# Two thirds of one unit's x turned by DMA, with earlier loads around it, in a fused attention and feed-forward kernel

## The chip, the cores and the metric

The kernel runs on one core of a Trainium2 chip. The core has five engines that run side by side, each working through its own stream of instructions in order: TensorE (PE in the profile; PEld is its weight load), VectorE (DVE), ScalarE (ACT), GpSimd (POOL) and SyncE (SP). Here SP does no arithmetic: it issues almost all DMAs, one after the other. The transfers themselves are done by 16 DMA engines that all queues share. The metric is the device time of one execution in microseconds (us). The kernel before takes 326.93 us, the median of three runs (326.87 to 327.19).

## The reference

Two stages. The first is attention with 4 batches, 8 heads, 768 tokens and head size 64, where a query sees only the keys with the same 6-bit hash. The second is a gated feed-forward layer on 3072 tokens of 512 values, with 1536 inner values.

```
q_bits = (q @ proj > 0);  k_bits = (k @ proj > 0)          # 6 bits each
mask   = q_bucket[:, None] == k_bucket[None, :]
attn   = softmax(where(mask, q @ k.T / 8, -1e9));  o = attn @ v
x      = o with the heads side by side                     # 3072 x 512
xn     = x / sqrt(mean(x * x) + 1e-6) * rms_g
out    = (silu(xn @ w_gate) * (xn @ w_val)) @ w_out
```

## The kernel before, in words

**Units and slots.** The work is cut into 8 units u of 384 tokens (batch u // 2, one half of its queries). Each unit has 8 heads, and each head three chunks, so a unit has NS = 24 slots. In slot t the main loop emits the scores of chunk t + 1 (line 349, TensorE into a PSUM bank s_ps), the exponentials of chunk t (line 361, ACT), and then whatever the plan holds for the slot: a list of closures that `at(window, slot, function, ...)` fills while the kernel is written out. So the order of instructions on every engine, SP's too, is the order of the slots and, within a slot, the order of the `at` calls. Nothing is reordered later. Units 0 and 1 are mixed: heads 0 and 1 of both come first, then heads 2 to 7 of unit 0, then those of unit 1. From slot 48 on it is unit after unit.

**Pairs.** Heads are prepared two at a time, as a pair (batch, hp). `load_natural` (line 97), `load_blocks` (line 120) and `load_v` (line 106) load a pair's q, k and v from memory into tiles of one pool of 8 buffers (tag "L"); a load waits until the former user of its buffer has been read. load_blocks reads rows of 32 floats, eight DMAs a pair. The pair is turned so that the head size lies on the partitions, on TensorE for batch 0 and pairs (1, 0) and (1, 1), on DVE (lines 188 and 195) for the rest. It is cast to half precision (lines 178 and 208) and hashed on TensorE (`hash_pairs`, `hash_one`). The signs of the hash, the bits, are copied by small DMAs on SP into rows 64 to 69 of the tile QK that the scores read (lines 277 and 308). v is cast by `v_prep` and summed by `v_sum` on POOL. `zero_rows` clears the upper half of a QK tile on POOL (line 146).

**Feed-forward.** When all heads of a unit have their output x (line 395), `norm` computes the reciprocal root (line 443, POOL) and scales x into xn in three thirds c of 128 tokens. Then xn is turned into xnT, of which the first layer's matmuls read all three thirds at once. There are two ways:

- `turn_x`: four TensorE transposes into a PSUM bank x_ps (line 467), then a multiply by the column of weights gcol into xnT on DVE (line 473). For this third norm scales by the root alone (line 460).
- `turn_dma`: one DMA transpose on SP (line 431). The weights must be in already, so norm multiplies by the row of weights `grow` as well (line 452). `grow` is loaded once, the same 2 KB to each of the 128 partitions (line 673), and multiplied by a constant on ACT (line 674).

`ONDMA` says how many thirds of a unit go by DMA: two for units 2 to 6, one for unit 7, none for units 0 and 1. Unit u's norm stands at slot 24 (u + 1) + 4, its DMA turns one slot later.

Then the gate and value matmuls (line 484, banks g_ps and v_ps) run over 12 blocks of 128 inner values, with a tanh on ACT (line 492) and two multiplies on DVE (lines 501 and 502) for each, and the projection of the former unit (line 513, y_ps), copied out by ACT (line 525) and stored by SP (line 526). `spread` lays these pieces over the slots of a unit by written-down weights. A third that goes by DMA keeps its weight as an empty piece there, except in the last unit. The weights wg, wv and wo are loaded by DMAs that POOL issues (line 585).

**What the planner sets for the bits.** `hash_one` is put into the plan by `spread`; the bits' DMAs follow in its slot, or in a later one if `SENDS` names it. `spots` gives for each pair from (1, 2) on the slot of its loads, of its turns, and of its hash.

The lines that set the slots of what is changed:

```python
    ONDMA = {2: 2, 3: 2, 4: 2, 5: 2, 6: 2, 7: 1}
    ...
    at(0, 60, nc.sync.dma_start, grow, moe_rms_g.partition_broadcast(128))
    at(0, 65, nc.scalar.mul, grow, grow, float(DMODEL) ** 0.5)
    ...
        for c in range(ONDMA.get(u, 0)):
            at(0, t0 + 5, turn_dma, u, c)
```

Of the kernel before, what the change touches and what calls it, by code (L numbers as in the profile page):

```python
# [19 lines left out]
DMODEL = H * D  # L20
# [13 lines left out]
def kernel(  # L34
# [12 lines left out]
    nc = tc.nc  # L47
# [27 lines left out]
    grow = const.tile([128, DMODEL], FP32, name="grow")  # L75
# [347 lines left out]

    rstds = {}

    ONDMA = {2: 2, 3: 2, 4: 2, 5: 2, 6: 2, 7: 1}

    def turn_dma(u, c):
        if c == 0:
# [16 lines left out]
    def norm(u):  # L446
# [3 lines left out]
        for c in range(3 if 0 < u < 7 else 2):  # L450
            if c < ONDMA.get(u, 0):
                nc.vector.scalar_tensor_tensor(
# [145 lines left out]
    def at(w, s, f, *a):  # L598
        plan[NS * w + s].append(lambda: f(*a))
# [70 lines left out]
    at(0, 1, load_natural, nc.sync, 0, 3, "q")  # L670
    at(0, 2, load_v, nc.sync, 0, 2)
    at(0, 2, load_v, nc.sync, 0, 3)
    at(0, 60, nc.sync.dma_start, grow, moe_rms_g.partition_broadcast(128))
    at(0, 65, nc.scalar.mul, grow, grow, float(DMODEL) ** 0.5)
    at(0, 6, v_prep, 0, 1)
    at(0, 15, v_prep, 0, 2)
    at(0, 19, v_prep, 0, 3, nc.vector)
# [6 lines left out]
        at(0, 39 + 3 * i, load_w, wo, moe_w_out, 6 * i, 6)  # L684


    for hp, ts in ((0, (8, 22, 23, 24, 25, 24, 39, 26, 28, 42)), (1, (20, 27, 28, 29, 30, 29, 41, 32, 33, 43))):
        tl, ts = ts[0], ts[1:]
        for w in "kq":
            at(0, tl, load_natural, nc.sync, 1, hp, w)  # L690
        at(0, tl, load_v, nc.sync, 1, hp)
        at(0, ts[0], new_pair, 1, hp)
        for t, hh, w in zip(ts[0:4], (0, 1, 0, 1), "kkqq"):
            at(0, t, turn_pe, 1, hp, hh, w)
        at(0, ts[4], cast_pool, 1, hp, "k")
        at(0, ts[5], cast_pool, 1, hp, "q")
        if hp == 0:
            at(0, ts[6], hash_pair, 1, hp)
            at(0, ts[7], send_pair, 1, hp)
        at(0, ts[8], v_prep, 1, hp)  # L700
        at(0, ts[8], v_sum, 1, hp)
# [1 line left out]
    spots = {  # L703
        (1, 2): (34, (48, 48), (46, 46), 51),
        (1, 3): (45, (55, 56), (57, 58), 61),
        (2, 0): (50, (63, 64, 65, 66), (67, 69, 70, 71), 73),
        (2, 1): (62, (72, 73, 75, 81), (82, 83, 84, 85), 86),
        (2, 2): (70, (87, 88, 89, 90), (91, 93, 94, 95), 97),
        (2, 3): (84, (96, 97, 99, 105), (105, 106, 106, 107), 108),
# [2 lines left out]
        (3, 2): (114, (135, 136, 137, 139), (140, 141, 142, 143), 145),  # L712
        (3, 3): (132, (144, 145, 147, 153), (153, 154, 154, 155), 156),
    }
    for i, t in ((0, 39), (1, 41), (2, 57), (3, 61)):
        at(0, t, zero_rows, i)
    TX = 37

# [16 lines left out]
    for n, (u, h) in enumerate(order):  # L735
        t = 3 * n + 4 - ((u, h) == (0, H - 1))
# [52 lines left out]
            inserts[2 * b * NS + s] = (MEAN, v_mean, b, hp, 4)  # L789


    SENDS = {(2, 0, 0): 77, (2, 0, 1): 77, (2, 2, 1): 101, (3, 2, 1): 149}

    def place(t, step):
        if step[0] is None:
# [2 lines left out]
        if step[0] is hash_one:  # L798
            late.append((t, hash_bits, *step[1:]))
            for pair in step[1:]:  # L800
                for hh in range(2):
                    s = SENDS.get((*pair, hh), t)
                    late.append((max(s, t), send_bits, *pair, hh))
# [26 lines left out]
    for u in range(7):  # L830
# [9 lines left out]
        at(0, t0 + 4, norm, u)  # L840
        for c in range(ONDMA.get(u, 0)):
            at(0, t0 + 5, turn_dma, u, c)
        pieces = []
        for i in range(9):
# [5 lines left out]
            if i in (6, 7):  # L850
                thirds = ((0,), (1, 2))[i - 6]
                for c in thirds:
                    if c >= ONDMA.get(u, 0):
                        pieces.append((TURN, False, [(0, turn_x, u, c)]))
# [10 lines left out]
    def behind_norm(t):  # L865

        return t - t % NS + 9 if 1 <= t % NS < 9 else t

    for (b, hp), (load, kturns, qturns, _) in spots.items():
        at(0, load, load_blocks, nc.sync, b, hp)  # L870
        at(0, load, load_v, nc.sync, b, hp)
        at(0, min(kturns + qturns), new_pair, b, hp)
        for w, turns in (("k", kturns), ("q", qturns)):
            for i, t in enumerate(turns):
                at(0, t, turn_dve, b, hp, w, i, len(turns))
            t = turns[-1] + 1
            at(0, t if (b, hp) == (1, 2) else behind_norm(t), cast_pool, b, hp, w)
        t = 54 if (b, hp) == (1, 2) else behind_norm(qturns[-1] + 2)
        at(0, t, v_prep, b, hp)
        at(0, t, v_sum, b, hp)  # L880

# [66 lines left out]
```

## Time and profile before

| | |
|---|---|
| median of three runs | 326.93 us |
| the profiled execution | 326.68 us |
| its span, first to last instruction | 324.9 us |
| granted TensorE clock | 0.999 |
| TensorE busy | 319.9 us, 98% of the span |
| ACT, DVE, POOL busy | 228.4, 229.7, 157.6 us |
| DMA | 32.63 MB moved, 85741 packets, 70908 of them under 512 bytes |

How to read it: the page has the busy time of each engine, then 40 slices of the span (8.1 us each), where a digit is the busy share in tenths. The chain follows the work that ended last back to its start. A timeline gives start, duration, engine, line, operation, output and input, and how many instructions are merged in the row; for SP (written SPq) a row is the issue of a DMA, not its transfer. Matmuls overlap on TensorE and their ends are modelled, so the distance between starts is what counts. The table of stretches gives the busy time of each engine in each stretch, the clock, the mean busy share of the 16 DMA engines (a little over 1 where packets overlap) and GB/s.

### The profile page before, as it was taken

The numbers are of one execution on the slowest core, as the hardware profiler recorded it, in microseconds if no ns is written. First come the engines' busy times: TensorE is split into PE (matmuls) and PEld (weight loads), VectorE is DVE, ScalarE is ACT, GpSimd is POOL, SyncE is SP. The second block draws the span as 40 slices with busy tenths as digits, with TensorE's granted clock in tenths as the row PEclk, the third lists the DMA queues.
The fourth block names the chain that finished last, engine by engine and source line by source line (L and its number), as shares of the span: only waits on it lengthen the run. The fifth ranks groups of instructions, "written<-read, shape, count | busy, mean of one in ns | idle before, by whom it ended". The sixth has DMA issues, their size and how long they took to land.

```text
span 324.9 us, 7772 instructions
## 1 busy us (share of the span) xinstructions
PE 319.9 (98%) x2955; PEld 194.4 (60%) x2955; DVE 229.7 (71%) x512; ACT 228.4 (70%) x333; POOL 157.6 (49%) x204
## 2 busy tenths in 40 slices
PE   8999999999999999999999999999999999999996
PEld 3676666656566565655566565655666556665554
DVE  5887876859888568874888568785677536673870
ACT  7999887667688676776767776777777768744322
POOL 4999759955974363731883621752582111221000
PEclk9999999999999999999999999999999999999999
DMA  7942999988428864055547056002100030003002
GB/s 208 360 168 85 226 216 195 192 159 151 103 38 158 157 136 88 6 94 156 89 100 145 35 125 120 7 5 66 72 4 3 1 99 34 0 2 105 10 2 97
DMA packets 85741, 32.63 MB, mean 100 GB/s; under 512 B 70908, under 2 KB 82632, under 8 KB 85704
## 3 DMA queue, kind: packets, MB, share of 16 engines
q1 hardware_dynamic: 81800, 27.35, 36.1%
q0 software_dynamic: 3680, 4.72, 8.5%
q8 instruction: 23, 0.38, 0.5%
q14 instruction: 14, 0.11, 0.1%
q10 hardware_dynamic: 224, 0.07, 0.1%
HBM read 28.58 MB, written 6.29 MB: 107 GB/s over the span
## 4 chain that ended last, share of the span: by engine, by line
PE 98%; ACT 1%; DVE 0%; issue 0%
PE s_ps L349 20%; PE g_ps L484 19%; PE v_ps L484 19%; PE y_ps L513 18%; PE o_ps L374 11%; PE d_ps L218 2%; PE t_ps L156 2%; PE d_ps L238 2%; PE z_ps L580 1%; PE x_ps L467 1%; PE y_ps L532 1%; PE m_ps L333 1%; ACT psb L361 1%; DVE kT L158 0%; PE s_ps L156 0%
## 5 line engine op out<-in xcount | busy, mean ns | idle before, releaser
L361 ACT ACTIVATE psb<-s_ps,ebias 128x768 f16<-128x768 f32 x192 | 167.7, 900 | 20.0 <-PE s_ps L349 19.2
L349 PE MATMUL s_ps<-QK 128*128 128x384 f16 (+1 forms) x384 | 93.5, 326 | 1.2 <-ACT psb L361 1.1
L492 ACT ACTIVATE t<-g_ps 128x384 f32<-128x384 f32 x96 | 47.2, 492 | 52.2 <-PE g_ps L484 50.5
L484 PE MATMUL g_ps<-xnT,wg 128*128 128x384 f16 x384 | 82.7, 326 | 0.0
L484 PE MATMUL v_ps<-xnT,wv 128*128 128x384 f16 x384 | 81.8, 326 | 0.0
L501 DVE SCALAR_TENSOR_TENSOR a<-t,g_ps 128x384 f32<-128x384 f32 x96 | 53.0, 552 | 28.9 <-ACT t L492 27.2
L395 POOL TENSOR_TENSOR x<-otmp,rcp 128x384 f32<-128x384 f32 x30 | 25.1, 837 | 96.2 <-DVE rcp L393 95.8
L513 PE MATMUL y_ps<-wo,ht 128*128 128x512 f16 x276 | 67.7, 379 | 0.0
L502 DVE SCALAR_TENSOR_TENSOR ht<-a,v_ps 128x384 f16<-128x384 f32 x96 | 53.2, 554 | 11.5 <-PE v_ps L484 3.6
L374 PEld LDWEIGHTS <-psb 128*128 128x128 f16 x1152 | 51.9, 97 | 15.7 <-issue 1.2
L374 PE MATMUL o_ps<-vl,psb 128*128 128x65 f16 x1152 | 55.8, 193 | 0.0
L349 PEld LDWEIGHTS <-QK 128*128 128x128 f16 (+1 forms) x384 | 34.8, 98 | 33.7 <-issue 7.9
L484 PEld LDWEIGHTS <-wg 128*128 128x128 f16 x384 | 35.2, 97 | 21.2
L484 PEld LDWEIGHTS <-wv 128*128 128x128 f16 x384 | 35.1, 97 | 20.8 <-issue 0.2
L513 PEld LDWEIGHTS <-ht 128*128 128x128 f16 x276 | 24.9, 98 | 23.0
L525 ACT COPY ysb<-y_ps 128x512 f32<-128x512 f32 x23 | 13.5, 587 | 15.8 <-PE y_ps L513 15.8
L388 DVE TENSOR_TENSOR otmp<-o_ps,cvb 128x390 f32<-128x390 f32 x32 | 17.8, 557 | 7.1 <-PE o_ps L374 7.1
L208 POOL CAST QK<-qT 64x768 f16<-64x768 f32 x20 | 16.5, 823 | 10.3 <-DVE qT L195 9.5
L401 POOL TENSOR_TENSOR sq<-x 128x384 f32<-128x384 f32 x24 | 19.9, 828 | 1.9
L208 POOL CAST QK<-kT 64x768 f16<-64x768 f32 x20 | 16.4, 822 | 5.2 <-DVE kT L195 3.1
L473 DVE TENSOR_TENSOR xnT<-x_ps,gcol 128x512 f16<-128x512 f16 x11 | 7.4, 688 | 15.1 <-PE x_ps L467 15.0
L195 DVE STREAM_TRANSPOSE kT<-kL 128x192 f32<-128x192 f32 x32 | 16.4, 516 | 0.0
(85 smaller groups left out, 274.9 us busy)
## 6 DMA issues: line engine op xcount, KB each, us to landing
vn<-in_v_dram SPq DMA_DIRECT2D x16, 384.0 KB
out_dram<-ysb SPq DMA_DIRECT2D x23, 256.0 KB
qL<-in_q_dram SPq DMA_DIRECT2D x40, 96.0 KB
kL<-in_k_dram SPq DMA_DIRECT2D x40, 96.0 KB
kn<-in_k_dram SPq DMA_DIRECT2D x5, 384.0 KB
qn<-in_q_dram SPq DMA_DIRECT2D x5, 384.0 KB
wg<-in_moe_w_gate_dram POOLq DMA_DIRECT2D x2, 768.0 KB, 9.4
wv<-in_moe_w_val_dram POOLq DMA_DIRECT2D x2, 768.0 KB, 11.7
```

Source lines behind the costliest of these rows:

```text
L208: nc.gpsimd.tensor_copy(QK[b, 2 * hp + hh, "h"][0:64, o : o + S], src[64 * hh : 64 * hh + 64, :])
L349: nc.tensor.matmul(ps[:, j, 0:HALF], QK[b, h, "h"][rows, S + jt * 128 : S + (jt + 1) * 128], QK[b, h, "h"][rows, half * HALF : (half + 1) ...
L361: nc.scalar.activation(psb[u, h][:, 2 * ch : 2 * ch + 2, :], sps.pop((u, i))[:, :, 0:HALF], AF.Exp, bias=ebias, scale=ESCALE,)
L374: nc.tensor.matmul(o[:, c, hh, 0:65], psb[u, h][:, jt, c * 128 : (c + 1) * 128], vls[b % 2][:, h, 2 * (jt % 3) + jt // 3 if b in PARITY el ...
L388: nc.vector.tensor_add(tmp[:, :, :, 0:65], o[:, :, :, 0:65], cvb[b % 2][:, 2 * hp : 2 * hp + 2, 0:65].unsqueeze(1).to_broadcast([128, 3, 2 ...
L395: eng.tensor_mul(xd.rearrange("p c (h d) -> p c h d", h=2), tmp[:, :, :, 0:64], r.to_broadcast([128, 3, 2, 64]),)
L401: eng.tensor_mul(sq, xd, xd)
L484: nc.tensor.matmul(ps, w[:, kt, fs], xnT[u][:, kt, :], start=(kt == 0), stop=(kt == 3))
L492: nc.scalar.activation(t, fbank[u, ft, "g_ps"], AF.Tanh, scale=0.5)
L501: nc.vector.scalar_tensor_tensor(out=a, in0=t, scalar=1.0, in1=g, op0=ALU.add, op1=ALU.mult)
L502: nc.vector.scalar_tensor_tensor(out=ht[u][:, ft, :], in0=a, scalar=0.5, in1=vv, op0=ALU.mult, op1=ALU.mult)
L513: nc.tensor.matmul(y, ht[u][:, ft, c * 128 : (c + 1) * 128], wo[:, ft, :], start=(ft == 0), stop=(ft == NF - 1),)
```

## The change

Seven things, all of them slots but the first:

- `ONDMA` gets unit 1: two of its three thirds are turned by DMA, in slot 53, and scaled by grow.
- grow, which unit 1 now needs, is loaded in slot 40 in place of 60, and multiplied in slot 49 in place of 65.
- The loads of pair (1, 1) go from slot 20 to slot 17, ahead of the bits of pair (0, 3).
- The loads of pair (2, 0) go from slot 50 to slot 49, which puts them ahead of the store of unit 0's first third.
- The zeroing of QK tile 3 goes from slot 61 to 69.
- The bits of pair (1, 2) are sent in slots 53 and 54, behind unit 1's DMA turns, in place of slot 51.
- v_prep and v_sum of pair (1, 2) go from slot 54 to 57.

```diff
-    ONDMA = {2: 2, 3: 2, 4: 2, 5: 2, 6: 2, 7: 1}
+    ONDMA = {1: 2, 2: 2, 3: 2, 4: 2, 5: 2, 6: 2, 7: 1}
...
-    at(0, 60, nc.sync.dma_start, grow, moe_rms_g.partition_broadcast(128))
-    at(0, 65, nc.scalar.mul, grow, grow, float(DMODEL) ** 0.5)
+    at(0, 40, nc.sync.dma_start, grow, moe_rms_g.partition_broadcast(128))
+    at(0, 49, nc.scalar.mul, grow, grow, float(DMODEL) ** 0.5)
...
-    for hp, ts in ((0, (8, 22, 23, 24, 25, 24, 39, 26, 28, 42)), (1, (20, 27, 28, 29, 30, 29, 41, 32, 33, 43))):
+    for hp, ts in ((0, (8, 22, 23, 24, 25, 24, 39, 26, 28, 42)), (1, (17, 27, 28, 29, 30, 29, 41, 32, 33, 43))):
...
-        (2, 0): (50, (63, 64, 65, 66), (67, 69, 70, 71), 73),
+        (2, 0): (49, (63, 64, 65, 66), (67, 69, 70, 71), 73),
...
-    for i, t in ((0, 39), (1, 41), (2, 57), (3, 61)):
+    for i, t in ((0, 39), (1, 41), (2, 57), (3, 69)):
...
-    SENDS = {(2, 0, 0): 77, (2, 0, 1): 77, (2, 2, 1): 101, (3, 2, 1): 149}
+    SENDS = {(1, 2, 0): 53, (1, 2, 1): 54, (2, 0, 0): 77, (2, 0, 1): 77, (2, 2, 1): 101, (3, 2, 1): 149}
...
-        t = 54 if (b, hp) == (1, 2) else behind_norm(qturns[-1] + 2)
+        t = 57 if (b, hp) == (1, 2) else behind_norm(qturns[-1] + 2)
```

On SP the order around the turns becomes: bits of (1, 1), grow, the loads of (1, 3), the loads of (2, 0), the store of unit 0's first third, the two DMA turns, four bits of (1, 2), a store, the other four bits, a store. TensorE loses eight transposes and keeps the order of everything else.

## The prediction

> **What bounds the kernel now.** I read the page first: busy time, slices, chain.
>
> ```profile
> PE 319.9 (98%) x2955; PEld 194.4 (60%) x2955; DVE 229.7 (71%) x512; ACT 228.4 (70%) x333; POOL 157.6 (49%) x204
> ...
> DMA  7942999988428864055547056002100030003002
> ...
> PE 98%; ACT 1%; DVE 0%; issue 0%
> ```
>
> TensorE works in order and without holes, so the time is the sum of its work plus any wait put into its stream. DVE, ACT and POOL have room. The DMA engines are full from about 32 to 81 us (slices 5 to 10, 8.1 us each): that is where the change adds a transfer and puts two urgent ones in the queue.
>
> Next TensorE's timeline where unit 1's x is turned (x_ps) and first used (g_ps), and, last two lines, the same place of unit 4, which turns two thirds by DMA already:
>
> ```profile
> 75.09 0.39 PE L467 MATMUL x_ps<-ident,xn 128*128 128x128 f16 x4
> 75.32 1.03 PE L513 MATMUL y_ps<-wo,ht 128*128 128x512 f16 x4
> ...
> 76.78 0.74 PE L467 MATMUL x_ps<-ident,xn 128*128 128x128 f16 x8
> 77.36 0.49 PE L349 MATMUL s_ps<-QK 128*128 128x384 f16 x2
> ...
> 78.82 0.49 PE L484 MATMUL g_ps<-xnT,wg 128*128 128x384 f16 x2
> ...
> 190.97 0.44 PE L374 MATMUL o_ps<-vl,psb 128*128 128x65 f16 x9
> 191.39 0.81 PE L484 MATMUL g_ps<-xnT,wg 128*128 128x384 f16 x4
> ```
>
> Starts count, not modelled ends. Four transposes take 0.23 us, the next eight 0.58 (0.13 of it a wait for a bank). The gate matmul at 78.82 is the first reader of unit 1's xnT: it stands in TensorE's order, and all scores, probabilities and projections behind it stand with it.
>
> Then SP's queue, which issues one DMA after the other; the last line is unit 4's pair of DMA turns:
>
> ```profile
> 70.23 0.39 SPq L526 DMA_DIRECT2D out_dram<-ysb  x1
> 70.72 3.46 SPq L120 DMA_DIRECT2D qL<-in_q_dram  x4
> 74.28 2.65 SPq L120 DMA_DIRECT2D kL<-in_k_dram  x4
> 77.04 0.58 SPq L106 DMA_DIRECT2D vn<-in_v_dram  x1
> 77.72 5.75 SPq L308 DMA_DIRECT2D QK<-bits  x8
> 83.58 0.86 SPq L526 DMA_DIRECT2D out_dram<-ysb  x2
> 84.49 0.46 SPq L599 DMA_DIRECT2D grow<-in_moe_rms_g_dram  x1
> ...
> 187.45 2.58 SPq L431 DMA_TRANSPOSE xnT<-xn  x2
> ```
>
> At 74 us, when unit 1's xn will be ready, SP is in the middle of pair (2,0)'s loads. Unit 4 gives the price of a DMA turn: first issue at 187.45, reader at 191.39, 3.94 us; the reader could have come at 191.24, as the nine short matmuls before it take 0.27, so it waited 0.15 us and 3.94 is the turn's own length.
>
> Last the stretches of the DMA (columns: busy us of each engine, clock, DMA share, GB/s):
>
> ```profile
> 26.00:30.50 4.50, 4.08 (x60) 3.25 (x58) 3.08 (x8) 4.50 (x6) 4.08 (x6) 1.00 0.07 14
> 30.50:34.00 3.50, 3.50 (x50) 2.33 (x49) 2.56 (x6) 2.87 (x5) 3.14 (x4) 1.00 1.02 336
> 34.00:42.00 8.00, 8.00 (x111) 5.44 (x110) 7.28 (x24) 7.52 (x9) 5.63 (x7) 1.00 1.14 196
> 59.50:64.40 4.90, 4.90 (x46) 3.07 (x45) 4.10 (x8) 3.32 (x6) 4.59 (x8) 1.00 1.18 196
> 64.40:72.00 7.60, 7.60 (x67) 3.89 (x66) 4.92 (x14) 5.56 (x8) 4.55 (x6) 1.00 0.84 132
> 86.00:88.50 2.50, 2.50 (x35) 1.24 (x32) 2.32 (x5) 1.49 (x2) 2.32 (x4) 1.00 0.63 103
> ```
>
> From 30.5 to 34 the loads of pair (1,1) run, then the weights; from 59.5 to 64.4 the last half of wo, in which SP's own queue moves next to nothing; 86 to 88.5 is grow alone.
>
> **Part 1, eight transposes off TensorE.** Twelve cost 0.23 + 0.58; four stay at 0.23. Saved 0.58 us, or 0.46 if the bank wait stays. Two multiplies out of PSUM (L473, 0.69 us each) leave DVE, and two xn go from L460 to L452 (0.75 us); DVE is not on the chain, nothing is saved there. The weights in the planner stay, so no other matmul moves.
>
> **Part 2, the turns' wait.** The two turns stand behind pair (2,0)'s vn and the store of (0,0). DVE is not what they wait for: the reciprocal root ends at 73.35, two L452 at 0.75 us end at 74.9. SP is. Before, vn's issue ends at 77.62. The store (0.49 with its gap) moves from in front of the (2,0) loads to behind them: nil for the turns. grow goes in ahead: its issue costs 0.5. Its transfer can cost more: by the trace's semaphore records the store before it landed at 86.57 and grow at 88.66, so it held the engines 2.1 us. The stretch 64.4 to 72 has 16% of 7.6 us free, 1.2 us, to swallow it in. I take 0.9, between 0.5 and 2.1. The Trainium skill ("DMA: Bandwidth & Descriptors", section on the anatomy of one DMA) fits a DMA issued by GpSimd as 2.0 us plus bytes over 436 GB/s, so 0.6 us of moving for grow's 256 KB. By that sentence the sum below would be 0.3 lower; no run here shows grow moving so fast.
>
> So the first turn is issued at 77.62 + 0.9 = 78.5 and the gate can start at 78.5 + 3.94 = 82.45. Without a wait it would start at 78.82 - 0.58 + 0.2 (part 3) = 78.45. The wait is 4.0 us, in TensorE's stream, and nothing behind it has a hole to give it back. Low end: if the weights start 0.8 us sooner (part 3) and grow costs 0.5, 2.8 us. High end: grow's whole 2.1, 5.2 us.
>
> **Part 3, pair (1,1) loaded from slot 17.** SP is idle from 23.97 (four bits from 21.12, 2.85 us) to 26.30; the three loads now go there, at about 24.0, 24.5 and 25.0, instead of 29.18 to 30.60. Their 1.18 MB leave a full stretch (30.5 to 34) for an empty one. But the weights were not waiting for them: POOL issues the first at 30.27 and its packets start at 33.6 by the trace's packet records, 3.3 us later, where the last half of wo, with no loads before it, takes 2.6 (56.66 to 59.3). So at most 0.8 us is gained, and that last half keeps its time, since POOL issues it at 56.66. I take none of it, and keep 0.8 for the low end. The bits of pair (0,3), issued at 26.30 as before, now follow these loads in the rings. Pair (1,0)'s loads landed up to 4.31 us after vn's issue, so this vn lands at 29.3; bits that came behind a load (pair (0,1)) landed 0.2 and 0.4 us after it. Then k and q bits land at 29.5 and 29.7, where scores of head 6 start at 29.36 and the q bits landed at 28.85 before. Bounds: 0 (pair (0,2)'s bits landed 1.9 us after issue although a load landed just before) and 0.65 (vn 4.56 after issue, as pair (1,1)'s own was). I take 0.2.
>
> **Part 4, what has cover.** grow's multiply on ACT (0.64 us) comes at 66.1: grow lands at 65.5 to 67.5, and a wait of 1.4 us ends before the scores of 69.66 need the bank; beyond 2 us it would show. Bits of (1,2): issued from 81.1 on (78.5 + 2.58), 0.7 us each, the first three landed by 84.3; scores of unit 2's head 4 now come at 82.34 - 0.4 + 4.0 = 85.9; cover 1.6. Bits of (1,3) and the later loads follow DVE and TensorE, which shift too. POOL: v_prep and v_sum of (1,2) (2.8 us) leave the idle time at 73.3 and fall behind a memset at 81.9, so (1,3)'s casts end 2.8 later, at 90.9, where scores read them at 91.9 before the wait is added; without the wait the margin is about 0.5, with it 4. The memset of slot 69 (2.65 us) was at 91.0 and goes later; scores read its tile from slot 102 on (149 us).
>
> **Sum.** 326.68 (profiled execution; 324.9 of it is span) - 0.58 + 0.2 + 4.0 = 330.3. That execution lies 0.25 under the median of 326.93, so about 330.5 as a median.
>
> **Rivals.** (a) The turns come in time. The place is SP at 74 us; it decides at a first turn issued by 78.45 - 3.94 = 74.5, 4.0 us sooner than I say. It would need the moved 1.18 MB to pull the whole queue forward (at 336 GB/s, 3.5 us) and grow to vanish in it. For it: the DMA is full for 45 us, and in a full stretch bytes taken away come back as time. Against: those bytes lay before the weights, not between them, and wo's last half is timed by POOL. Time: 326.68 - 0.58 + 0 to 0.2, plus 0.25: 326.35 to 326.55, and slightly faster or the same by the measurement, which tells 0.2% (0.65 us) from no change. (b) The queue comes forward part of the way, by 1.5 to 3 us: wait 1 to 2.5, 327.5 to 329. (c) More is late: grow's 2.1 us in full, or longer as its reads meet wo's, the store's 256 KB in the rings ahead of the turns as well (0.7), or the bits of (0,3) at 0.65: 332.2 to 333.5.
>
> **How the numbers follow.** The order in SP's queue is certain, and it was busy until 77.62; so my case (wait 2.8 to 5.2, 329.3 to 331.7) gets 0.73, (a) 0.10, (b) 0.08, (c) 0.09. The range 327.9 to 332.3 leaves out (a) and most of (c). Slower: 0.73 + 0.08 + 0.09 = 0.90; of (a), 0.03 faster and 0.07 the same.
>
> **What would show it.** Right: in TensorE's timeline a hole of some 4 us before the first g_ps of unit 1, and four x_ps matmuls in front of it in place of twelve; SP's queue with the pair of turns at 78 to 79, directly after the store behind vn; ACT and DVE idle at 79 to 82; nothing else new past 85 us. Loads of (1,1) at 24 to 25.4 and the weights' packets starting no sooner than 32.8. A hole of 0.2 us before the scores at 29.4. Wrong: turns issued by 75 us, which would mean that the queue was held by those loads after all; or a hole elsewhere, at 29 us (bits), 67 us (ACT waiting for grow) or 91 us (POOL's casts).

## The result and the profile after

The changed kernel takes 334.39 us (median of four runs, 333.06 to 335.45); the kernel before, beside it on the same chip, 326.96. The ratio is 1.0218, with a 95% interval of 1.0200 to 1.0236. The forecast was 330.5, with a range of 327.9 to 332.3: the direction was right, the size was not. The profiled execution of the changed kernel took 333.79 us, its span is 332.0.

First the page of the changed kernel: busy time, three rows of its slices (8.3 us each), the chain, and from the groups the gate's matmuls with their idle time in front.

```profile
PE 322.0 (97%) x2947; PEld 195.0 (59%) x2947; DVE 227.7 (69%) x510; ACT 228.0 (69%) x333; POOL 156.9 (47%) x204
...
PE   9998999995899999999999999999999999999996
...
PEclk9999999999799999999999999999999999999999
DMA  7945999999105948026475237101300030002002
...
PE 95%; ACT 2%; DMA 1%; DVE 1%; issue 0%; DVEq 0%
...
L484 PE MATMUL g_ps<-xnT,wg 128*128 128x384 f16 x384 | 83.5, 328 | 4.4 <-DMA xnT<-xn 4.4
```

TensorE has eight matmuls less and yet 2.1 us more of busy time (322.0 against 319.9). The slices say why: the digit 5 at 75 to 83 us is the expected hole, and in the slice behind it the granted clock is 7 in place of 9. TensorE's timeline at that place shows both:

```profile
77.63 0.39 PE L467 MATMUL x_ps<-ident,xn 128*128 128x128 f16 x4
...
78.46 1.03 PE L513 MATMUL y_ps<-wo,ht 128*128 128x512 f16 x4
83.85 0.79 PE L484 MATMUL g_ps<-xnT,wg 128*128 128x384 f16 x2 [4.37 <-DMA xnT<-xn]
84.43 0.85 PE L349 MATMUL s_ps<-QK 128*128 128x384 f16 x2
85.07 0.85 PE L484 MATMUL g_ps<-xnT,wg 128*128 128x384 f16 x2
```

Four x_ps matmuls are left of twelve, as the change says. The projection's four matmuls are through at 79.31 (they are 0.21 us apart), and the gate starts at 83.85: a hole of 4.54 us. Behind it two matmuls of 384 columns take 0.64 us of starts (84.43 to 85.07) where they take 0.33 otherwise. The table of stretches for the hole, for what follows, and for the time after that (the columns are as before: us, PE, PEld, DVE, ACT, POOL, clock, DMA share, GB/s):

```profile
79.30:83.85 4.55, 0.18 (x1) 0.03 (x1) 1.55 (x4) 0.63 (x2) 3.42 (x3) 1.00 0.96 199
84.30:87.50 3.20, 3.20 (x13) 1.48 (x11) 0.82 (x2) 1.28 (x2) 2.98 (x5) 0.53 0.24 88
87.50:91.50 4.00, 4.00 (x41) 2.64 (x40) 3.34 (x6) 2.28 (x4) 2.03 (x4) 1.00 0.20 72
```

By the trace's clock records TensorE is granted half its clock from 83.90 to 87.32. SP's queue shows where the turns stand:

```profile
74.88 2.66 SPq L120 DMA_DIRECT2D kL<-in_k_dram  x4
77.64 0.58 SPq L106 DMA_DIRECT2D vn<-in_v_dram  x1
78.32 0.41 SPq L526 DMA_DIRECT2D out_dram<-ysb  x1
78.83 2.72 SPq L431 DMA_TRANSPOSE xnT<-xn  x2
```

Directly behind vn and the store, as forecast. By the trace's semaphore records vn landed at 82.02, the store at 82.76, the turns at 83.28 and 83.72. The bits of pair (0, 3) left a smaller hole in front of the scores of head 6, which started at 30.43 in place of 29.36.

To compare the two profiled executions I took the start of each slot's scores in both and noted where the distance between them changes:

| term | forecast | measured |
|---|---|---|
| start-up, first scores 6.86 to 7.29 | none | +0.42 |
| wait for the bits of (0, 3) | +0.2 | +0.69 |
| eight transposes | -0.58 | -0.57 |
| wait of unit 1's gate | +4.0 | +4.54 |
| half clock behind that wait | none | +1.68 |
| end of the program, behind the last matmul | none | +0.37 |
| sum | +3.6 | +7.1 |

The spans differ by 7.1 and the execution times by 7.11. The start differs by 0.25 to 1.10 us in the traces of all the variants below, whatever was changed; I count it as chance. SP's queue has a chance of its own on top of that. The run `end_two` below is the kernel before up to 248 us, and yet its v of pair (2, 0) was issued at 79.23 where the kernel before issued it at 77.04: 2.19 us later, with a start of TensorE only 1.10 later. So a difference of about 1 us between the holes of two single traces can be chance, and below it is called so.

### The profile page after: what moved, and what is told of

Its sections match the earlier page's. It is cut to its first block, busy times and chain, and to the rows that moved or that the text cites. A ratio compares the mean times of both kernels' runs of the same rounds, so it can differ in the third digit from the quotient of the medians.

```text
span 332.0 us, 7760 instructions
## 1 busy us (share of the span) xinstructions
PE 322.0 (97%) x2947; PEld 195.0 (59%) x2947; DVE 227.7 (69%) x510; ACT 228.0 (69%) x333; POOL 156.9 (47%) x204
## 4 chain that ended last, share of the span: by engine, by line
PE 95%; ACT 2%; DMA 1%; DVE 1%; issue 0%; DVEq 0%
PE s_ps L349 19%; PE g_ps L484 19%; PE v_ps L484 19%; PE y_ps L513 18%; PE o_ps L374 10%; PE d_ps L218 2%; PE t_ps L156 2%; PE d_ps L238 2%; ACT psb L361 1%; PE z_ps L580 1%; DMA xnT<-xn 1%; PE y_ps L532 1%; PE x_ps L467 1%; PE m_ps L333 0%; PE s_ps L156 0%
## 5 line engine op out<-in xcount | busy, mean ns | idle before, releaser
L473 DVE TENSOR_TENSOR xnT<-x_ps,gcol 128x512 f16<-128x512 f16 x9 | 6.1, 690 | 16.4 <-PE x_ps L467 16.4
```

## Experiments

The theory: TensorE waits for the turns, which come late because of what stands ahead of them in SP's queue; and the wait costs more than its length, since it is followed by half clock. The rivals: the matmuls behind the wait are slow for another reason (the transfers just landed, the banks); the turns are late because the DMA engines are full, not because of the order in the queue; something else that the change does sets the time.

**The half clock.** The changed kernel, with 17 matmuls of ones put in front of unit 1's first gate matmul. They write the next of the three banks that x_ps, y_ps, g_ps and v_ps take in turn, and nobody reads the result:

```diff
+            if u == 1:
+                warm = bank("z_ps")
+                idle(17, lambda name: warm)
```

> The changed kernel with 17 matmuls of ones (512 columns, 0.22 us each, 3.7 us in all, result not used) on TensorE directly before the first gate matmul of unit 1, where the changed kernel stands still for 4.54 us. After that hole its matmuls of 384 columns start 320 ns apart in place of 162 for some 3.4 us (granted clock 0.59 from 84 to 88 us), which costs 1.6 to 1.7 us. Theory A, the half speed comes from TensorE having been idle: the gate still starts when the DMA turns have landed, some 0.8 us of hole is left, but the half speed is gone, and the kernel is 1.7 us faster than the changed one, about 332.5 us. Rival B, the half speed has another cause (the DMA traffic, or this place of the program): it stays, and the time is that of the changed kernel, 333 to 335.5 us.

Measured 331.68 (331.63 to 332.07), ratio to the kernel before 1.0135 [1.0121, 1.0149], 2.7 us under the changed kernel. TensorE's timeline at the gate:

```profile
79.51 3.88 PE L583 MATMUL z_ps<-const-bfloat16-1.0 128*128 128x512 bf16 x17
83.34 0.48 PE L484 MATMUL g_ps<-xnT,wg 128*128 128x384 f16 x2
83.67 0.49 PE L349 MATMUL s_ps<-QK 128*128 128x384 f16 x2
```

and the stretch that answers to the slow one above:

```profile
83.50:87.50 4.00, 4.00 (x41) 2.63 (x40) 2.35 (x4) 2.37 (x4) 3.78 (x5) 1.00 0.21 75
```

The gate waits just as before, but TensorE is kept busy, the clock stays at 1.00, and scores are 0.33 us apart. The scores move by 3.83 us at this place where they moved by 6.21. Half clock after an idle TensorE is shown; the transfers and their order were the same, and the banks were taken in the same turn, one further on. The time lies 0.8 below what A expected: the profiled gate came 0.5 us sooner as well (83.34 for 83.85), which the fillers do not explain and which is within the chance of the queue. So of the 2.7 us some 1.7 belong to the clock.

**The order in SP's queue.** The changed kernel, with pair (2, 0)'s loads behind the turns and the bits of (1, 2), and its k issued before its q:

```diff
...
-        (2, 0): (49, (63, 64, 65, 66), (67, 69, 70, 71), 73),
+        (2, 0): (54, (63, 64, 65, 66), (67, 69, 70, 71), 73),
```

> The changed kernel with the loads of pair (2,0) in slot 54 in place of 49, so that they stand behind the DMA turns and the bits of (1,2) in SP's queue, and with that pair's k issued before its q. Theory A, the turns are late because SP and the rings are busy with these loads: first turn issued at about 75.5 us in place of 78.8, the gate no more than 0.6 us late, no half speed; 326.7 - 0.6 + 0.7 (bits of pair (0,3), as in the changed kernel) + 0 to 0.6, so 326.9 to 327.6 us. Rival B, a DMA turn is slow here for itself (rings full of other loads up to 76 us): the hole stays at 2 us or more, over 329 us.

Measured 332.44 (331.82 to 333.79), 1.0164 [1.0139, 1.0188]. The turns were issued at 75.31 and 76.74, both had landed by 79.17, and the gate did not wait: 3.86 us from first issue to last landing. So A was right at the gate; the time is nevertheless above 329, not for B's reason but because the lateness moved on. SP's queue in this kernel:

```profile
84.43 2.72 SPq L120 DMA_DIRECT2D kL<-in_k_dram  x4
87.25 2.66 SPq L120 DMA_DIRECT2D qL<-in_q_dram  x4
...
91.20 5.99 SPq L307 DMA_DIRECT2D QK<-bits  x8
```

TensorE's timeline there, and then the stretch behind it:

```profile
95.54 0.48 PE L348 MATMUL s_ps<-QK 128*128 128x384 f16 x2 [3.01 <-DMA QK<-bits]
```

```profile
97.00:100.00 3.00, 3.00 (x11) 1.37 (x9) 1.54 (x3) 1.32 (x3) 0.00 (x0) 0.50 0.42 66
```

Now the bits of (1, 3) stand behind the moved loads, scores wait 3.2 us for them, and half clock follows again.

**The early loads of (1, 1), alone.** The kernel before with nothing but slot 20 made 17:

> The kernel before with one change, the loads of pair (1,1) in slot 17 in place of 20. Theory A, as the trace of the changed kernel reads: a hole of 0.69 us before the scores of head 6 at 29.4 to 30.4 us, because the bits of pair (0,3) land behind the loads, and nothing given back: 327.6 us, 0.2% slower. Rival B, the weights and with them the rest of the queue come so much sooner that it is made up: 326.9 us or less.

Measured 328.23 (327.26 to 330.65, 12 runs) against 327.36, 1.0032 [1.0015, 1.0048]. The one new hole is 0.90 us before the scores of head 6; nothing later comes sooner. In this kernel, the changed one and its variants with slot 17 and grow in slot 40 this wait is 0.69 to 0.90, above the upper bound of 0.65 that I gave it.

**grow, first try.** The changed kernel with grow loaded in slot 20 in place of 40:

> The changed kernel with the load of grow in slot 20 in place of 40, where SP is idle and the DMA engines have not begun on the weights. It shows what grow costs the turns. If it costs its issue alone (0.5 us), the first turn is issued at 78.3 in place of 78.83 and the hole is 4.0 in place of 4.54; if its whole transfer (2.1 us), the first turn is issued at 76.8 and the hole is 2.5. The prediction took 0.9: hole 3.6. If the half speed after the hole needs a hole of a certain length, it may go here, for 1.7 us more: 330 to 333 us.

Measured 333.44 (332.88 to 334.07), 1.0186 [1.0170, 1.0203]. This is over what was expected, and it did not isolate grow: its transfer met the loads of (1, 1) and the bits of (0, 3), which landed at 31.6 to 32.2, so a hole of 2.03 us opened there, with half clock from 32.84 to 36.26. At the gate 2.78 us were left, with no half clock behind them (why, the last section says).

**The early loads undone in the changed kernel**, slot 17 back to 20:

> The changed kernel with the loads of pair (1,1) back in slot 20. Theory A (these loads in slot 17 only cost): the hole of 0.7 to 0.9 us before the scores of head 6 goes, the hole before the gate matmuls of unit 1 stays at 4.5 us (4 to 5.2), and so does the half speed after it: 0.8 us faster than the changed kernel, 333.2 to 333.8. Rival B (they also bring the queue forward): the hole before the gate grows by as much as they brought, up to 0.8 us, and the time is that of the changed kernel, 334.4.

Measured 334.78 (332.14 to 335.29), 1.0214 [1.0183, 1.0246]: no gain is seen, but this interval takes in the 0.8 us of A as well, so the time does not decide. The trace does in part. The hole at 29 us is gone, but the one before the gate is 5.97 us: TensorE comes to it 0.8 us sooner, and the turns land 0.6 us later (83.83 and 84.32), which alone would be within the chance of the queue. Half clock lasts longer too (2.5 us lost). A wait early in TensorE's stream is given back at a later one that is set by the queue.

**grow, second try**: the kernel just shown, with grow in slot 17, where SP is idle.

> As the run before, and grow loaded in slot 17 (SP idle at 24 to 26 us, DMA engines at 2 to 7%) in place of 40. It shows what grow costs the turns where nothing else moves. If its issue alone: the hole before the gate goes from 4.5 to 4.0 us. If its whole transfer: to 2.4. The prediction's middle value, 0.9: to 3.6. A hole of 0.1 to 0.5 at 29 us may come with it, since the bits of pair (0,3) follow grow. With the half speed 332 to 332.8 us, without it 330.5 to 331.5.

Measured 334.40 (332.83 to 335.27), 1.0214 [1.0190, 1.0238]. The hole before the gate is 5.26 in place of 5.97, and none opens at 29 us. The lengths expected were reckoned from the changed kernel's 4.5, while the kernel this one starts from has 5.97; what could tell is the difference of 0.7. But the turns land at 83.86 and 84.32, where they landed without the move (83.83 and 84.32), and TensorE's start is 0.71 later by chance, which is the whole difference. So neither try shows what grow costs ahead of the turns; with the chance of the queue at about 1 us, one trace each cannot.

**The loads divided.** The last kernel, with (2, 0)'s q left in front of the turns, then the turns, four bits of (1, 2), k, the other four bits, and v in slot 58:

```diff
...
+        split = (b, hp) == (2, 0)
-        at(0, load, load_blocks, nc.sync, b, hp)
-        at(0, load, load_v, nc.sync, b, hp)
+        at(0, load, load_blocks, nc.sync, b, hp, "q" if split else "qk")
+        if split: at(0, 53, load_blocks, nc.sync, b, hp, "k")
+        at(0, 58 if split else load, load_v, nc.sync, b, hp)
```

> As the run before, and pair (2,0)'s loads divided around the turns in SP's queue: q in slot 49, then the turns and four bits of (1,2), then k, the other four bits, v in slot 58, and then the bits of (1,3). Theory A (the whole loss at the gate is what stands ahead of the turns in SP's queue and in the rings): first turn issued at 75 to 75.5, gate waits 0 to 0.8 us, no half speed, bits of (1,3) as early as before: 326.4 to 327.3 us beside 326.9 to 327.4 of the kernel before, no measurable difference; the eight transposes saved (0.57 us) are about what is won. Rival B: a hole of 2 us or more stays at the gate or turns up at the scores of pair (1,3), over 329 us.

Measured 327.76 (326.61 to 330.23, 12 runs) against 327.38, 1.0019 [1.0002, 1.0035]. Against the kernel shown last, 6.6 us come back from the order in one queue alone, with the same bytes to move. The turns were issued 4.63 us sooner (75.15 for 79.78) and took 4.02 us to the gate in place of 4.67, while the DMA engines were busy for 0.72 of that time in place of 0.92. So most of the lateness is the place in the queue; full DMA engines are the smaller part of it. Left are a hole of 0.55 at the gate and one of 0.31 at 88 us.

**The turns in another engine's queue.** The changed kernel with slot 20, unit 1's turns issued by ACT in slot 55:

```diff
-        nc.sync.dma_start_transpose(
+        (nc.scalar if u == 1 else nc.sync).dma_start_transpose(
...
```

> The changed kernel with pair (1,1) in slot 20, and unit 1's two turns issued by ACT in slot 55 instead of SP in 53; SP's queue is as long as in the changed kernel. ACT reaches slot 55 at about 75.6 us. If only the place in SP's queue is late: turns issued at 75.6 and 76.9, landed by 79.3, hole before the gate 1 us, no half speed, 327.5 to 328.5 us. If the DMA engines themselves are what is late (full from 72 to 81 us): landing after 81, hole 2.5 us or more, 329.5 to 332 us. ACT is held 2.5 us by the issue itself, which delays the scores' bank at 79 us by up to 0.5 us in either case.

Measured 332.80 (331.76 to 333.02), 1.0160 [1.0141, 1.0178], over both forecasts. The turns were issued at 75.83 and 77.46 and landed by 80.27, and the gate's hole is 0.83, as if only the queue had been late. But in the trace's semaphore records SP then stands: a load of kL, queued at 76.40, waits for a DMA semaphore that one of ACT's turns is using, and goes on at 79.89, 0.02 us after that turn landed. The bits of (1, 2) behind it come late, and TensorE shows it:

```profile
86.61 0.48 PE L349 MATMUL s_ps<-QK 128*128 128x384 f16 x2 [2.52 <-DMA QK<-bits]
```

The hole is 2.69 us, with half clock behind it (87.40 to 90.82). A further 0.86 us of this execution is a wait at 68 us for the second half of wo, which stands in no other trace.

**The divided loads, tightened**: the store behind the turns, the turns a slot earlier, k behind all eight bits of (1, 2).

> The divided loads once more, with the two holes left in them attacked: the store of unit 0's first third goes from in front of the DMA turns to behind the bits of (1,2), the turns go one slot earlier, and the second load of (2,0) goes behind all eight bits of (1,2). In the divided kernel the store's issue ended at 75.05 with the turns at 75.15 and a hole of 0.55 us before the gate, and the bits of (1,2) from 85.25 left 0.31 us before scores at 88.0. Theory A (only what stands ahead in SP's queue makes the holes): turns issued at about 74.5, second one landed by 78.5, no hole at the gate and none at 88 us; the whole saving of 0.57 us is left, less chance at the start of up to 0.5: 326.4 to 327.1, against about 327.4 for the kernel before. Theory B (the turns and the bits stay late because the DMA engines are full, or because xn is ready no sooner): the holes stay at 0.3 to 0.6 each, or a new one opens where k of (2,0) is turned: 327.4 or more.

Measured 327.87 (326.95 to 329.50, 12 runs) against 327.14, 1.0021 [1.0005, 1.0037]. Both holes are gone. A new one of 0.71 stands at the next transfer:

```profile
92.45 0.48 PE L348 MATMUL s_ps<-QK 128*128 128x384 f16 x2 [0.67 <-DMA QK<-bits]
```

**The end of the program.** In the kernels shown so far the last store has landed 0.91 us before the end where unit 1 is not turned by DMA (two kernels), and 1.28 us before it where it is (nine). So, the kernel before with two DMAs of 256 bytes added in an idle place:

```diff
...
+    for i in range(2):
+        at(0, 168, nc.sync.dma_start, scr[:, 64 * i : 64 * i + 64], moe_rms_g[0:64].partition_broadcast(1))
```

> The kernel before, with nothing changed but two small DMAs (256 bytes each, into a scratch tile that nobody reads) on SP at about 248 us, where SP and the DMA engines are idle. In every kernel with unit 1's two extra DMA turns the time from the landing of the last store to the end of the program is 1.28 us, in the two without them 0.91. The trace shows SP at the end waiting for the DMA semaphores one after the other, in a fixed order of eight, 0.065 us each, and DMAs use the eight in turn: in the kernel before the last store has the last of the eight, in the others the second. Theory A (two DMAs more turn the round, and six waits then come behind the last landing): the end takes 1.28 us here too, the span is 0.37 longer, time 0.3 to 0.5 over the kernel before beside start-up chance. Theory B (it is something else that the change does): 0.91 as before, same time.

Measured 327.51 (327.02 to 328.15, 12 runs) against 327.15, 1.0008 [0.9999, 1.0016]. The time cannot tell 0.37 us from nothing, but the trace can: the last store landed at 325.08 and the end came at 326.37, 1.29 later. At the end SP passes the eight DMA semaphores one after the other, 0.065 us each; with two DMAs more the last store no longer has the last of them but the second, and six passes follow. So two DMAs more do it, whether they are turns or loads of 256 bytes.

**Both together**: the tightened kernel, v behind the bits of (1, 3), and six such small DMAs.

> The divided loads of the run before, with v of (2,0) moved from slot 58 to 62, behind the bits of (1,3), and with six small DMAs (256 bytes each into a scratch tile that nobody reads) on SP at about 248 us. The run before had one hole left, 0.71 us at 92.45 before scores, since the bits of (1,3) came behind that v; and its end took 1.28 us from the last landing. Six more DMAs should bring the last store back to the last of the eight semaphores. Theory A (queue order and the round of semaphores are all that is left between the saving of 0.57 us and the time): no hole of over 0.3 us from 74 to 100 us, end 0.91, span 324.4 to 325.2 with the start as it falls, time 326.2 to 327.0, at or below the kernel before by 0.1 to 0.6. Theory B (the stretch from 74 to 94 us has no room for the two turns): a hole of 0.5 or more opens again at the next transfer, 327 or more.

Measured 327.31 (326.53 to 328.38, 12 runs) against 327.15, 1.0002 [0.9991, 1.0013]. The end is back at 0.91. The hole at 92 us is gone, but 0.91 us stands at unit 1's gate again (its queue ran later from 73 us on, though no edit against the kernel just before stands ahead of that, and the turns were issued at 76.06; this is the chance of the queue), and 0.50 at 117 us before unit 2's gate, whose turns landed at 117.26, 1.7 us later than in the kernel just before, behind loads that were issued later. The lateness found the next user a third time; how much of it is chance here stays open. No variant beat the kernel before; the most that there is to win is 0.57 us.

## Why the prediction was wrong, step by step

- **Part 1, the transposes: right.** 0.57 measured for 0.58. The cover on DVE was free.
- **Part 2, the order in SP's queue: right.** The first turn was forecast for 78.5 and was issued at 78.83, with TensorE's start 0.42 later by chance; that it came so close is in part luck, as the queue alone moves by about 1 us. The loads of (1, 1) did not pull the queue forward enough to matter, so rival (a) fell. The 0.9 taken for grow is not shown: with grow moved away the turns landed at the same time (84.32 in both traces), and the two differ by chance at the start.
- **Part 2, the length of a turn: too short.** 3.94 us came from unit 4, whose turns met nearly empty queues. Here it took 5.02 from first issue to the gate: vn and the store, issued just before, landed at 82.02 and 82.76, and the turns came out behind them. The DMA engines were busy for 0.95 of this time; in the two variants where the loads stood elsewhere it was 0.39 and 0.72, and the turns took 3.86 and 4.02. I had the store's share (0.7) in rival (c) and should have had it in the sum. In the profiled execution TensorE was also 0.86 us later at the gate than I had forecast (79.31 for 78.45), which swallowed most of it: the hole was 4.54, inside the bounds of 2.8 to 5.2.
- **Part 2, "The wait is 4.0 us, in TensorE's stream, and nothing behind it has a hole to give it back": this is the step that failed.** It prices a wait at its own length. The half clock behind it cost another 1.68 us in the profiled execution, and no term, bound or rival held it. The forecast for the profiled execution was 330.3, and it took 333.79. Of the 3.5 us between them the half clock is 1.68; the gate's wait adds 0.54 over its 4.0, the bits of (0, 3) 0.49, the start 0.42 and the end 0.37. So it is the largest single miss, and about half of the whole: the median of 334.39 less 1.68 is 332.7, still 0.4 above the range. (With TensorE kept busy through the wait 331.68 was measured, with a queue that was earlier by chance.) The trace of before had a hint: TensorE's first matmuls of 512 columns stand 0.43 us apart at 1 to 3 us, twice the 0.21 of later ones, and the kernel itself runs filler matmuls there (line 580). The Trainium skill ("TensorE: Matmul & The Clock Gate", section "Part 1: The HAM clock gate") says that after an idle window of about 3.4 us the clock falls to half, and stays there until a window has been busy. The hole of 4.54 us, with TensorE busy for 0.05 of the 3.41 us ahead of the change, and the 3.41 us of half clock agree with that; the forecast wait of 4.0 us was not weighed against it. A window that is idle in part can be enough, as the last section shows.
- **Part 3, the bits of (0, 3): mis-sized.** 0.2 taken, 0.65 as the upper end, 0.69 measured here and 0.90 in the loads moved alone. Alone it costs 0.3% [0.15, 0.48]. In the changed kernel the gate's wait took it up: undoing it made that wait longer, and no gain was measured.
- **Part 4, the cover: right.** No hole at 67 us, at the bits of (1, 2) or at POOL's casts; nothing new past 88 us but the end.
- **Not in the sum at all: 0.37 us at the end**, by two DMAs more. It is small, but set against a saving of 0.57 it is most of it.

## What to carry to other kernels

A wait of some microseconds in the stream of a TensorE that is otherwise full is to be priced at its length plus what the half clock behind it costs (here 1.5 to 2.5 us), and filler matmuls in the wait take that second part away (here 17). Work taken off TensorE and given to an in-order DMA queue has to be priced in that queue: first when the queue gets there, then how full the queues are that it lands behind, and then who stands behind it; moving the other transfers away only makes the next user late, three times here. Where a saving is under a microsecond, the fixed ends count as well, such as the round of DMA semaphores.

## What the runs showed that I had not expected

- The length of the hole alone did not decide on the half clock. Holes of 2.03, 2.69, 3.18, 4.54, 5.26 and 5.97 us brought it, one of 2.78 us did not, nor did any under 1 us. What decides is how a hole lies against a grid. In all thirteen traces the changes of the granted clock that are on record lie whole multiples of 3.41 us apart, and the grid begins at another point of the program in each. The two longest holes of grow's first try show both cases, cut at that grid (columns as before, the second is TensorE's busy time):

```profile
29.43:32.84 3.41, 1.54 (x27) 1.34 (x26) 0.61 (x2) 1.41 (x3) 2.31 (x3) 1.00 0.69 172
32.84:36.26 3.42, 3.42 (x27) 2.56 (x23) 1.66 (x4) 2.38 (x3) 2.33 (x3) 0.50 1.02 164
...
80.63:84.05 3.42, 1.91 (x27) 1.04 (x23) 2.79 (x5) 2.35 (x3) 0.70 (x1) 1.00 1.03 243
84.05:87.46 3.41, 2.31 (x16) 1.43 (x17) 0.55 (x1) 1.14 (x2) 3.27 (x3) 1.00 0.31 86
```

The hole of 2.03 us falls into one window of the grid and leaves 1.54 us of it busy: the next window is at half clock. The hole of 2.78 us is divided between two windows, each of which stays busy for 1.91 us or more: the clock stays. The other windows of the thirteen traces agree: at full clock, half clock followed each window in which TensorE was busy for 1.54 us or less, and none in which it was busy for 1.70 us or more. Half clock ended behind a window that was busy throughout. Two windows that were busy for 0.49 and 1.79 us did not end it, so in the kernels with holes of 5.26 and 5.97 us it lasted 6.83 us, and it began while TensorE still waited. An estimate from these rows: a hole of 3.8 us leaves at least one of two neighbouring windows with no more than 1.5 us busy wherever it falls, so the forecast wait of 4.0 would have brought half clock in any execution, and one of 2.8, the low end, in some only. By the page of the Trainium skill named above a gap would have to reach about 3.4 us; by these runs 2.0 can be enough.
- Queues of different engines are tied by the DMA semaphores that they share: a turn on ACT held SP for 3.5 us.
- Executions with the hole spread more (333.06 to 335.45) than those of the kernel before beside them (326.87 to 327.19). But so do two kernels without it: the early loads alone (327.26 to 330.65) and the divided loads (326.61 to 330.23), where the kernel before beside them took 326.68 to 328.42. The cause was not looked for.
